# Second chunk's triangles out and back during the first solver, wider stages for the early weights, solver in slots 8 to 33, merges at slots 5 and 12

## The chip, the cores and the metric

The kernel runs on one core of a Trainium2 chip. The metric is the device time of one execution in microseconds (us). A core has five engines that each work through a list of their own in order: TensorE (PE in the profile, with its weight loads as PEld), VectorE (DVE), ScalarE (ACT), GpSimd (POOL) and SyncE (SP), which here does little but issue DMAs. An engine waits where its next instruction needs something that another engine or a DMA has not finished.

## The reference

Three layers follow one another. The first is a recurrence with a 40x40 state for each of 32 heads (4 batches x 8 heads) over 768 tokens; the other two are perceptrons over the 3072 tokens of its output.

```python
def _attn_ref(r, k, v, w, a, b):
    state = np.zeros((B, H, D, D)); y = np.zeros_like(r)
    for t in range(S):
        kt, vt, rt = k[:, :, t], v[:, :, t], r[:, :, t]
        wt, at, bt = w[:, :, t], a[:, :, t], b[:, :, t]
        y[:, :, t] = np.einsum('bhd,bhde->bhe', rt, state)
        Sa = np.einsum('bhde,bhe->bhd', state, at)
        state = state * wt[:, :, None, :] - np.einsum('bhd,bhe->bhde', Sa, bt) \
              + np.einsum('bhd,bhe->bhde', vt, kt)
    return y
...
x = attn_out.transpose(0, 2, 1, 3).reshape(3072, 320)
x = np.maximum(x @ w_in, 0.0) ** 2 @ w_out          # layer 0: 320 x 2048, 2048 x 320
h = x @ w_in2
out = (h * np.cos(h)) @ w_out2                       # layer 1
```

The perceptrons' weights arrive as 64-bit floats.

## The kernel before

**The recurrence in chunks.** The 768 tokens are cut into 12 chunks of 64. Within a chunk the recurrence becomes dense products with a triangular matrix of 64x64 per head, which must be inverted. `decay` makes the running products of `w`; `compact_kb` and `compact_a` lay k, b and a out; `gt` multiplies them on TensorE and VectorE masks the products into the tiles `ga`. `gt_out` writes the triangles in `ga` to DRAM (`Ls`, SyncE), `solve_load` fetches their diagonal blocks of 32x32 back, one per partition, into `L` (and the unit matrix `kti` into `T`), and `solve` inverts these 128 blocks: 31 steps of a product and a sum, 62 instructions, and a copy (line 517). I call this the **solver**; it runs on VectorE for chunk 0 and on GpSimd for the others. `solve_store` writes the result to DRAM (`Tn`, `Ts`), `load_t` fetches it in two layouts (`t_120`, which the trace shows as `t`, and `tt`), and `merge` joins the 32x32 blocks into 64x64 with products of `t`, `tt` and the corner block `l21` (loaded by `corner_load`; `l_119`, or `l`, in the trace): TensorE's `pw`, ACT's copy, `pt`, ACT's copy into `tt`, once for each half of the heads. `state` then runs a chunk's four groups of heads: `px` uses the triangles in `ga`, `pu` the merged `tt`, and the state goes on in `mov`, `mt` and `M0d`. In chunk 0, `pmat` fills parts of `mov` with zeros.

**The order.** It is written out by hand. `Program.run` writes the prologue, with chunk 0's solver on VectorE: a wrapper, `Vector`, puts one solver instruction behind each other instruction of VectorE while it has credit. Then `period(c)` is called for c = 0 to 11. A period is 42 slots; a table, `at(slot, function)`, says what is issued in which slot. Period c runs `state` of chunk c, the solver of chunk c + 1 (`rate[t]` of its instructions in slot t), and decay, layout and triangles of chunk c + 2. Each engine works in the order in which its instructions were issued, so the slot says who stands in front of whom on each engine; it says no time.

**The weights.** A 64-bit float is taken apart into two 32-bit words: ACT clamps (`clamp`), VectorE cuts the bits out (`bits`), GpSimd adds the low word (`add`, line 183, into `u`), and `split` makes a high and a low part on ACT and GpSimd (line 215, into `ws`). `first` does 12 early tiles of layer 0 whole (`w1`); a job's steps stand at numbered stages, and jobs start five stages apart. `rest` and `second` do the other tiles in `pieces` (`w2`, three for each tile) from period 2. The profile shows a step's tile by its number.

**The perceptrons.** Layer 0 is fed from period 2 on, a yield at a time, between the slots: `h` on TensorE, `g`, `gh` and `gl` on ACT and GpSimd (`gl` at line 766), `po` on TensorE. From about 863 us on there is only layer 1.

Of the kernel before, what the change touches and what calls it, by code (L numbers as in the profile page):

```python
# [158 lines left out]
class Weights:  # L159
# [58 lines left out]
    def first(self, last=NF, layer=0):  # L218
# [3 lines left out]
        def job(f):  # L222
# [9 lines left out]
            def begin(c0, n):  # L232
                u = st[c0] = m.p2.tile([128, 512], F32, tag="g", name="u1", bufs=3)[:, 0:n]
                if self.raw:
                    self.clamp(st["w"][:, c0:c0 + n], u)
                else:
                    self.nc.sync.dma_start(u, self.i[nm][f, :, c0:c0 + n])

            out = [(0, load)]
            for t, c0, n in ((5, 0, 384), (6, 384, DM)):  # L240
                out.append((t, lambda c0=c0, n=n: begin(c0, n)))
                if self.raw:
                    out += [(t + 1, lambda c0=c0, n=n: self.bits(st["w"][:, c0:c0 + n], st[c0])),
                            (t + 2, lambda c0=c0, n=n: self.add(st["w"][:, c0:c0 + n], st[c0], st[c0]))]
                out.append((t + 4, lambda c0=c0: self.split(st["dst"], st[c0], c0, layer)))
            return out
# [3 lines left out]
    def pieces(self, nm, tiles, period, end):  # L250
# [4 lines left out]
        def job(f, c0, n):  # L255
            st = {}

            def load():
                st["w"] = self.p.tile([128, 256, 2], I32, tag="w", name="w", bufs=2)[:, 0:n]
                self.load(nm, f, st["w"], c0)  # L260

            def clamp():
                st["u"] = self.p.tile([128, 256], F32, tag="u", name="u", bufs=2)[:, 0:n]
                self.clamp(st["w"], st["u"])

            return [(0, load), (4, clamp), (6, lambda: self.bits(st["w"], st["u"])),
                    (7, lambda: self.add(st["w"], st["u"], st["u"])), (period + 5, lambda: end(f, c0, st["u"]))]
# [40 lines left out]
class Attn:  # L308
# [274 lines left out]
    def pmat(self, c, g):  # L583
# [18 lines left out]
        for r0, n, s0 in ((64, 40, 0), (0, 64, 4)):  # L602
            if c:
                nc.scalar.activation(mov[r0:r0 + n, s0:s0 + 4, 64:104], self.MT[g][r0:r0 + n], AF.Copy)
            else:
                nc.gpsimd.memset(mov[r0:r0 + n, s0:s0 + 4], 0.0)

# [6 lines left out]

    def state(self, c, g):
        nc = self.nc
        ga, rv, mov = self.ga[c, g // 2], self.rv.pop((c, g)), self.mov.pop((c, g))
# [41 lines left out]
        if not last:  # L659
            self.vec.tensor_tensor(mt[0:104], yv[0:104, :, 64:104], mt[0:104], op=ALU.add)  # L660
        if c:
            self.vec.tensor_tensor(sz[0:104], yv[0:104, :, 0:64], sz[0:104], op=ALU.add)
        if not last:
            self.vec.tensor_tensor(mt[0:104], mt[0:104],
                                   self.lam[(c + 1) % 3][:, 4 * g:4 * g + 4, 64:65].to_broadcast([104, 4, 40]), op=ALU.mult)
        if g % 2 == 0:
# [282 lines left out]


FIRST, RATE = 9, 64.2 / 42


class Program:
# [59 lines left out]
    def run(self):  # L1014
# [57 lines left out]
        for k in range(10):  # L1072
            self.vec.credit = 6
            step(g1, 2 if k > 7 else 1)
            if k == 6:
                A.gt_out(1, 0, 0)
                A.gt_out(1, 0, 1)
            if k in (1, 3, 4, 5, 6, 7):
                step(self.w1)
# [24 lines left out]
    def period(self, c):  # L1104
# [9 lines left out]
        for half in range(2):  # L1114
            for k in range(5):
                for q in range(2):
                    at(20 * half + 4 * k, step, st[2 * half + q])
        for h, t0 in enumerate((5, 5) if c == 0 else (2, 2) if more else (4, 12)):
            mg = A.merge(h)
            at(t0, step, mg)  # L1120
            at(t0 + (4 if c and more else 2), step, mg)
        at(2, A.rv_load, c, 2)
        at(6, A.rv_load, c, 3)
        at(6, A.mov_load, c, 2)
        at(8, A.pmat, c, 2)
        at(14, A.mov_load, c, 3)
        at(16, A.pmat, c, 3)
        at(17, A.y_store, c, 0)
        at(37, A.y_store, c, 1)
        if more:  # L1130
# [9 lines left out]
            if c:  # L1140
                at(6, A.solve_load, c + 1)
            at(8 if c == 0 else 6, A.corner_load, c + 1)
            first, last = (2, 26) if c == 0 else (9, 36)
            for t in range(first, last):
                rate[t] = 3 if t % 3 == 0 or c == 0 else 2
            rate[last] = 100
            at(28 if c == 0 else 37, A.solve_store)
            at(30 if c == 0 else 38, A.load_t)
            at(23, A.rv_load, c + 1, 0)
# [138 lines left out]
```

## Time and profile before

| | |
|---|---|
| median of 3 runs | 1274.33 us (1273.46 to 1278.36) |
| the profiled execution: its time, its span | 1272.46 us, 1270.7 us |
| mean granted clock of TensorE | 0.916 |
| busy: PE, PEld | 1065.8 us (84%), 894.4 us (70%) |
| busy: DVE, ACT, POOL | 696.7 us (55%), 697.6 us (55%), 690.3 us (54%) |
| DMA | 115.96 MB, mean 91 GB/s |

The span is the time from the first instruction's start to the last one's end in the trace; the execution's own time is 1.76 us longer. Busy shares are means over stretches that have different limits, so they don't tell what bounds a stretch. In a row of the timeline the first number is the time from the start of the span, the second the duration; the operation, output and inputs follow, and a bracket at the end gives how long the engine was idle before the instruction and what ended that. A row with `SPq` is an issue in SyncE's queue, and its duration is that of issuing, not of the transfer.

### The profile page before, as it was taken

The numbers are of one execution on the slowest core, as the hardware profiler recorded it, in microseconds if no ns is written. First come the engines' busy times: TensorE is split into PE (matmuls) and PEld (weight loads), VectorE is DVE, ScalarE is ACT, GpSimd is POOL, SyncE is SP. The second block draws the span as 40 slices with busy tenths as digits, with TensorE's granted clock in tenths as the row PEclk, the third lists the DMA queues.
The fourth block names the chain that finished last, engine by engine and source line by source line (L and its number), as shares of the span: only waits on it lengthen the run. The fifth ranks groups of instructions, "written<-read, shape, count | busy, mean of one in ns | idle before, by whom it ended". The sixth has DMA issues, their size and how long they took to land.

```text
span 1270.7 us, 26720 instructions
## 1 busy us (share of the span) xinstructions
PE 1065.8 (84%) x10242; PEld 894.4 (70%) x10242; DVE 696.7 (55%) x1315; ACT 697.6 (55%) x1444; POOL 690.3 (54%) x1106
## 2 busy tenths in 40 slices
PE   3334636889889885989698989999999999999997
PEld 3334535667767764867577867777889999999996
DVE  7955964666657572666466634123696343443432
ACT  4223634566466554656456556547756555655553
POOL 3157693776638381838384838226796333333332
PEclk9996665888889897989799989999999999999999
DMA  8545726446372817463736362236101010101000
GB/s 197 126 100 144 178 82 123 104 97 150 60 172 64 166 44 160 101 140 73 167 92 145 69 133 74 59 99 210 68 19 46 1 47 1 47 9 38 1 21 24
DMA packets 267621, 115.96 MB, mean 91 GB/s; under 512 B 225036, under 2 KB 246028, under 8 KB 266652
## 3 DMA queue, kind: packets, MB, share of 16 engines
q1 hardware_dynamic: 265650, 113.47, 37.2%
q8 instruction: 83, 1.36, 0.4%
q10 hardware_dynamic: 1834, 0.69, 0.2%
q14 instruction: 54, 0.44, 0.1%
HBM read 88.42 MB, written 25.69 MB: 90 GB/s over the span
## 4 chain that ended last, share of the span: by engine, by line
PE 55%; POOL 18%; DVE 7%; DMA 7%; SPq 5%; issue 3%; ACT 3%; POOLq 0%; ACTq 0%; DVEq 0%
PE h L913 23%; PE pt L857 13%; PE po L867 9%; POOL T L513 5%; POOL ttmp L510 5%; DMA xf<-xs 3%; POOL gl L766 3%; POOL u L183 2%; PE pgt L459 2%; POOL ws L215 2%; DVE lam L146 2%; DVE u L146 1%; PE pu L644 1%; PE py L654 1%; DVE cin L146 1%
## 5 line engine op out<-in xcount | busy, mean ns | idle before, releaser
L913 PE MATMUL h<-xh,ws 128*128 128x512 f32 x960 | 328.8, 405 | 17.6 <-ACT g L763 17.0
L766 POOL TENSOR_TENSOR gl<-g,gh 128x512 fp32r<-128x512 f32 x96 | 126.0, 1313 | 201.5 <-ACT gh L765 150.4
L913 PE MATMUL h<-xl,ws 128*128 128x512 f32 x576 | 232.1, 403 | 0.2 <-DVE xl L146 0.2
L794 POOL TENSOR_TENSOR gl<-g,gh 128x512 fp32r<-128x512 f32 x96 | 125.1, 1303 | 190.9 <-ACT gh L793 161.5
L913 PEld LDWEIGHTS h<-xh,ws 128*128 128x128 f32 x960 | 182.4, 191 | 60.9 <-ACT g L763 21.6
L510 POOL TENSOR_TENSOR ttmp<-T,L 128x126 f32<-128x126 f32 (+22 forms) x310 | 123.6, 399 | 55.4 <-DMA L<-Ls 22.2
L867 PE MATMUL po<-gh,ws 128*128 128x512 f32 x480 | 142.9, 422 | 3.3 <-ACT o L813 2.7
L513 POOL TENSOR_TENSOR T<-T,ttmp 128x126 f32<-128x126 f32 (+22 forms) x310 | 132.1, 426 | 19.5
L857 PE MATMUL pt<-ws,gh 128*128 128x320 f32 x768 | 128.2, 309 | 0.5 <-DVE g L146 0.4
L763 ACT ACTIVATE g<-h 128x512 f32<-128x512 f32 x96 | 57.1, 594 | 129.5 <-PE h L913 106.8
L857 PEld LDWEIGHTS pt<-ws,gh 128*128 128x128 f32 x768 | 120.0, 188 | 8.3 <-DVE g L146 0.6
L913 PEld LDWEIGHTS h<-xl,ws 128*128 128x128 f32 x576 | 110.2, 191 | 20.7 <-DVE xl L146 1.4
L146 DVE SCALAR_TENSOR_TENSOR g<-n,h 128x512 f32<-128x512 int32 x96 | 65.9, 687 | 104.2 <-ACT n L774 101.7
L774 ACT ACTIVATE n<-h 128x512 int32<-128x512 f32 x96 | 57.3, 596 | 119.4 <-PE h L913 119.4
L146 DVE TENSOR_TENSOR mov<-pu,kc 64x416 f32<-64x416 f32 x96 | 56.5, 589 | 111.6 <-PE pu L645 99.1
L867 PEld LDWEIGHTS po<-gh,ws 128*128 128x128 f32 x480 | 93.4, 200 | 27.1 <-ACT o L813 3.3
L146 DVE TENSOR_TENSOR g<-g,h 128x512 f32<-128x512 f32 x96 | 65.8, 686 | 71.1 <-ACT g L778 71.0
L459 PE MATMUL pgt<-at,cin 40*128 40x104 f32 x768 | 71.0, 328 | 30.3 <-POOL at L439 12.8
L146 DVE TENSOR_SCALAR u<-u 128x160 f32<-128x160 f32 (+9 forms) x144 | 56.2, 391 | 64.0 <-ACT u L171 59.3
L459 PEld LDWEIGHTS pgt<-at,cin 40*128 40x128 f32 x768 | 61.5, 229 | 36.5 <-POOL at L439 13.5
L867 PE MATMUL po<-gl,ws 128*128 128x512 f32 x288 | 86.6, 405 | 0.0
L183 POOL TENSOR_TENSOR u<-u,w 128x384 int32<-128x384 int32 (+2 forms) x72 | 56.1, 779 | 53.7 <-DVE u L146 33.7
(112 smaller groups left out, 2310.3 us busy)
## 6 DMA issues: line engine op xcount, KB each, us to landing
w<-moe SPq DMA_DIRECT2D x20, 704.0 KB
rv<-rv SPq DMA_DIRECT2D x48, 256.0 KB
cin<-cin SPq DMA_DIRECT2D x8, 832.0 KB
Ls<-ga SPq DMA_DIRECT2D x48, 128.0 KB
L<-Ls SPq DMA_DIRECT2D x44, 128.0 KB
mov<-vt SPq DMA_DIRECT2D x96, 40.0 KB
xs<-yt SPq DMA_DIRECT2D x48, 80.0 KB
w<-moe SPq DMA_DIRECT2D x24, 160.0 KB
```

What stands on the lines that cost most here:

```text
L146: fn(*args, **kwargs)
L183: self.nc.gpsimd.tensor_tensor(t.bitcast(I32), u.bitcast(I32), w[:, :, 0], op=ALU.add)
L459: nc.tensor.matmul(pv[par][:, j], self.kb[r0:r0 + 40, p0 + j].rearrange("p h b -> p (h b)"), self.at[r0:r0 + 40, p0 + j], start=True, stop ...
L510: eng.tensor_tensor(tv, T[:, 0:r, j:j + 1].to_broadcast([128, r, n]), L[:, j:j + 1, j + 1:32].to_broadcast([128, r, n]), op=ALU.mult)
L513: eng.tensor_tensor(T[:, 0:r, j + 1:32], T[:, 0:r, j + 1:32], tv, op=ALU.add)
L763: nc.scalar.activation(g, h, AF.Relu)
L766: self.later.append((2, lambda: nc.gpsimd.tensor_tensor(gl, g, gh, op=ALU.subtract)))
L774: nc.scalar.activation(n, h, AF.Copy, bias=0.25, scale=float(np.float32(1.0 / (2.0 * np.pi))))
L794: nc.gpsimd.tensor_tensor(gl, g, gh, op=ALU.subtract)
L857: nc.tensor.matmul(self.pos[j][:, 0:DM], x[:, 128 * j:128 * j + 128], wo[:, DM * ws:DM * ws + DM], start=(f == 0 and x is gh and ws == 0), ...
L867: nc.tensor.matmul(self.pos[m], wo[:, 128 * ws:128 * ws + 128], x, start=(f == 0 and k in (0, 2, 4)), stop=(f == NF - 1 and k in (5, 6, 7)))
L913: nc.tensor.matmul(h, wi[:, ws], x[:, kt], start=(k == 0), stop=(k == 7))
```

## The change

It has six parts.

- `first`: the load of an early tile stands two stages later, `bits` and `add` one stage later, `split` four stages later. The first 384 columns of the 32-bit value go into a tile of the tag `gl` instead of `g`.
- `pieces`: the load of a piece stands one stage later.
- Prologue: `gt` of chunk 1 advances two steps per round from the start of chunk 0's solver, so that its last `ga` is made about half way through it. `gt_out` of chunk 1's second half and `solve_load(1)` are issued there and no longer behind `load_t`.
- The zero fills of `pmat` for groups 2 and 3 of chunk 0 go from GpSimd to VectorE.
- `state`: the multiplication of `mt` by the decay comes ahead of the sum for `y`.
- The table of a period: the solver in slots 8 to 32 at 8 instructions in 3 slots, the remainder in 33 (before: 9 to 35 at 7 in 3, the remainder in 36), its stores and loads in 34 and 36 (37 and 38); merges at 5 and 12, three slots between the two halves of each (2 and 2 with four slots between; in period 0 5 and 5); the first two groups' `state` steps at 0, 4, 10, 14 and 18 (0, 4, 8, 12, 16), `load_kb` in 6 (1), and several loads and layouts a few slots later.

```diff
@@ first
-                u = st[c0] = m.p2.tile([128, 512], F32, tag="g", name="u1", bufs=3)[:, 0:n]
+                if c0 == 0 and self.raw:
+                    u = st[c0] = m.p2.tile([128, 512], F32R, tag="gl", name="u0", bufs=3).bitcast(F32)[:, 0:n]
+                else:
+                    u = st[c0] = m.p2.tile([128, 512], F32, tag="g", name="u1", bufs=3)[:, 0:n]
...
-            out = [(0, load)]
+            out = [(2, load)]
...
-                    out += [(t + 1, lambda c0=c0, n=n: self.bits(st["w"][:, c0:c0 + n], st[c0])),
-                            (t + 2, lambda c0=c0, n=n: self.add(st["w"][:, c0:c0 + n], st[c0], st[c0]))]
-                out.append((t + 4, lambda c0=c0: self.split(st["dst"], st[c0], c0, layer)))
+                    out += [(t + 2, lambda c0=c0, n=n: self.bits(st["w"][:, c0:c0 + n], st[c0])),
+                            (t + 3, lambda c0=c0, n=n: self.add(st["w"][:, c0:c0 + n], st[c0], st[c0]))]
+                out.append((t + 8, lambda c0=c0: self.split(st["dst"], st[c0], c0, layer)))
@@ pieces
-            return [(0, load), (4, clamp), (6, lambda: self.bits(st["w"], st["u"])),
+            return [(1, load), (4, clamp), (6, lambda: self.bits(st["w"], st["u"])),
@@ pmat
-                nc.gpsimd.memset(mov[r0:r0 + n, s0:s0 + 4], 0.0)
+                (nc.gpsimd if g < 2 else self.vec).memset(mov[r0:r0 + n, s0:s0 + 4], 0.0)
@@ state (the same multiplication of mt stood behind the sum into sz)
+            self.vec.tensor_tensor(mt[0:104], mt[0:104],
+                                   self.lam[(c + 1) % 3][:, 4 * g:4 * g + 4, 64:65].to_broadcast([104, 4, 40]), op=ALU.mult)
         if c:
             self.vec.tensor_tensor(sz[0:104], yv[0:104, :, 0:64], sz[0:104], op=ALU.add)
@@ run
-            step(g1, 2 if k > 7 else 1)
-            if k == 6:
+            step(g1, 2)
+            if k == 4:
                 A.gt_out(1, 0, 0)
                 A.gt_out(1, 0, 1)
+            if k == 7:
+                A.gt_out(1, 1, 0)
+                A.gt_out(1, 1, 1)
+                A.solve_load(1)
...
         A.solve_store()
         A.load_t()
-        A.gt_out(1, 1, 0)
-        A.gt_out(1, 1, 1)
-        A.solve_load(1)
@@ period
-                    at(20 * half + 4 * k, step, st[2 * half + q])
+                    at(t, step, st[2 * half + q])
-        for h, t0 in enumerate((5, 5) if c == 0 else (2, 2) if more else (4, 12)):
+        for h, t0 in enumerate((5, 12)):
...
-            at(t0 + (4 if c and more else 2), step, mg)
+            at(t0 + 3, step, mg)
...
-            first, last = (2, 26) if c == 0 else (9, 36)
+            first, last = (2, 26) if c == 0 else (SOLVE, END)
             for t in range(first, last):
-                rate[t] = 3 if t % 3 == 0 or c == 0 else 2
+                rate[t] = 2 if c and t % 3 == 0 else 3
             rate[last] = 100
-            at(28 if c == 0 else 37, A.solve_store)
-            at(30 if c == 0 else 38, A.load_t)
+            at(28 if c == 0 else END + 1, A.solve_store)
+            at(30 if c == 0 else END + 3, A.load_t)
...
-                at(1, A.load_kb, c + 2)
+                at(6, A.load_kb, c + 2)
```

How the instructions stand is shown at two places of SyncE's queue. The first is the prologue, from the loads of chunk 1's inputs to those that period 0 uses. `Ls<-ga` is `gt_out`, `lent<-kti` and `lent<-Ls` are `solve_load`, `Tn` and `Ts` are `solve_store`, `t_120` and `tt` are `load_t`, `w_...<-moe` is an early tile's load. Before:

```order
L473 DMA Ls<-ga 64x8x64 x2
L187 DMA w_419<-moe 128x1408
L524 DMA Tn<-L 64x512
L526 DMA Ts<-T 1024x1x32 x2
L533 DMA t_120<-Tn 32x32x16 x2
L539 DMA tt<-Ts 32x16x32 x4
L473 DMA Ls<-ga 64x8x64 x2
L493 DMA lent<-kti 128x512
L496 DMA lent<-Ls 32x32x32 x4
L573 DMA rv<-rv 128x512 x2
```

Now:

```order
L187 DMA w_378<-moe 128x1408
L476 DMA Ls<-ga 64x8x64 x4
L496 DMA lent<-kti 128x512
L499 DMA lent<-Ls 32x32x32 x4
L527 DMA Tn<-L 64x512
L529 DMA Ts<-T 1024x1x32 x2
L536 DMA t_120<-Tn 32x32x16 x2
L542 DMA tt<-Ts 32x16x32 x4
L187 DMA w_504<-moe 128x1408
L576 DMA rv<-rv 128x512 x2
```

The second half of chunk 1's triangles and their way back moved ahead of the stores of chunk 0's solver, and an early weight tile moved from ahead of these stores to behind `load_t`.

The second place is between two solvers on GpSimd, at the turn from period 3 to period 4, from the end of one `load_t` to the next `solve_load`. `cin<-cin` is `load_kb`, `mov<-vt` is `mov_load`, `T<-kti` and `L<-Ls` are `solve_load`. Before:

```order
L473 DMA Ls<-ga 64x8x64
L187 DMA w<-moe 128x320
L379 DMA cin<-cin 104x2048
L573 DMA rv<-rv 128x512
L187 DMA w<-moe 128x320
L473 DMA Ls<-ga 64x8x64 x2
L573 DMA rv<-rv 128x512
L581 DMA mov<-vt 64x4x40 x2
L493 DMA T<-kti 128x512
L496 DMA L<-Ls 32x32x32 x4
L501 DMA l_119<-Ls 32x16x32 x2
```

Now:

```order
L187 DMA w<-moe 128x256
L476 DMA Ls<-ga 64x8x64
L187 DMA w<-moe 128x320
L576 DMA rv<-rv 128x512
L476 DMA Ls<-ga 64x8x64 x2
L187 DMA w<-moe 128x320
L576 DMA rv<-rv 128x512
L584 DMA mov<-vt 64x4x40 x2
L496 DMA T<-kti 128x512
L499 DMA L<-Ls 32x32x32 x4
L382 DMA cin<-cin 104x2048
```

`cin<-cin` moved from ahead of the triangles' store to behind their load, and `l_119<-Ls` left this stretch for a later one.

## Rows read from the trace of the kernel before

**Rows 1.** Table of stretches: window, length, engines' busy us (instructions), PEclk, DMA share, GB/s.

```profile
410.00:476.00 66.00, 56.74 (x709) 45.02 (x707) 41.59 (x87) 36.47 (x83) 42.08 (x77) 0.95 0.47 104
476.00:546.00 70.00, 55.99 (x700) 45.52 (x701) 34.61 (x68) 39.18 (x88) 39.58 (x76) 0.88 0.53 118
863.00:1271.00 408.00, 398.79 (x2149) 356.29 (x2148) 198.24 (x281) 233.64 (x388) 190.01 (x165) 0.99 0.12 41
```

**Rows 2.** Waits of PE, 340 to 810: for whom, total us, count, longest.

```profile
PE pw L550 <- DMA t<-Tn: 37.8, 14, 9.2
PE pu L644 <- ACT tt L567: 14.9, 4, 7.4
```

**Rows 3.** Timeline of PE: the first product of two successive merges.

```profile
416.23 0.28 PE L550 MATMUL pw<-t,l 32*32 32x32 f32 x2 [5.14 <-DMA t<-Tn]
481.48 0.28 PE L550 MATMUL pw<-t,l 32*32 32x32 f32 x2 [9.22 <-DMA t<-Tn]
```

**Rows 4.** Timeline of POOL: first products and closing copies of solvers.

```profile
77.17 0.24 POOL L510 TENSOR_TENSOR lent<-lent 128x31 f32<-128x31 f32 x1 [22.01 <-DMA lent<-Ls]
...
114.76 1.34 POOL L517 COPY lent<-lent 64x512 f32<-64x512 f32 x1
...
146.21 0.24 POOL L510 TENSOR_TENSOR ttmp<-T,L 128x31 f32<-128x31 f32 x1 [0.52 <-DMA L<-Ls]
...
200.31 1.05 POOL L517 COPY L<-T 64x512 f32<-64x512 f32 x1
...
409.81 1.13 POOL L517 COPY L<-T 64x512 f32<-64x512 f32 x1
...
435.69 0.27 POOL L510 TENSOR_TENSOR ttmp<-T,L 128x31 f32<-128x31 f32 x1 [4.96 <-DMA l<-Ls]
...
474.90 1.31 POOL L517 COPY L<-T 64x512 f32<-64x512 f32 x1
...
795.72 1.12 POOL L517 COPY L<-T 64x512 f32<-64x512 f32 x1
```

**Rows 5.** Timeline of SyncE's queue between the solvers of chunks 5 and 6.

```profile
419.01 0.35 SPq L379 DMA_DIRECT2D cin<-cin  x1
...
419.87 1.52 SPq L473 DMA_DIRECT2D Ls<-ga  x2
...
429.36 3.95 SPq L496 DMA_DIRECT2D L<-Ls  x4
```

**Rows 6.** Timeline, prologue: end of the first solver, and the issue behind it.

```profile
60.25 0.59 DVE L517 COPY L<-T 64x512 f32<-64x512 f32 x1
...
66.68 2.26 SPq L473 DMA_DIRECT2D Ls<-ga  x2
```

**Rows 7.** Timeline of DVE: two sums of the first solver.

```profile
42.97 0.92 DVE L513 TENSOR_TENSOR T<-T,ttmp 128x126 f32<-128x126 f32 x1
...
46.79 0.29 DVE L513 TENSOR_TENSOR T<-T,ttmp 128x126 f32<-128x126 f32 x1
```

**Rows 8.** Groups of POOL, 60 to 116: count, busy us, mean ns, idle before.

```profile
L215 POOL TENSOR_TENSOR ws<-u,ws 128x256 fp32r<-128x256 f32 (+2 forms) x8 | 4.3, 555 | 0.0
L183 POOL TENSOR_TENSOR u<-u,w 128x320 int32<-128x320 int32 (+1 forms) x4 | 3.9, 962 | 0.0
L606 POOL MEMSET mov<- 40x416 f32 (+1 forms) x4 | 1.8, 455 | 0.2
```

**Rows 9.** Timeline of DVE, period 0: first `pu` product and last `ga` of chunk 2.

```profile
81.91 1.21 DVE L146 TENSOR_TENSOR mov<-pu,kc 64x416 f32<-64x416 f32 x2 [11.78 <-PE pu L645]
...
135.42 1.06 DVE L146 TENSOR_TENSOR ga<-pgt,kc 128x416 f32<-128x416 f32 x2
```

**Rows 10.** Groups of POOL within one solver run, 435.7 to 476.2.

```profile
L766 POOL TENSOR_TENSOR gl<-g,gh 128x512 fp32r<-128x512 f32 x6 | 7.7, 1276 | 0.0
L183 POOL TENSOR_TENSOR u<-u,w 128x160 int32<-128x160 int32 (+2 forms) x3 | 1.8, 606 | 0.0
```

**Rows 11.** Waits of all engines, 200 to 870: ACT for pieces of weights.

```profile
ACT u L171 <- DMA w<-moe: 6.3, 4, 3.7
```

More of the change, by code (lines that the diff above doesn't have):

```diff
@@ L660, in state @@
             self.vec.tensor_tensor(mt[0:104], yv[0:104, :, 64:104], mt[0:104], op=ALU.add)
+            self.vec.tensor_tensor(mt[0:104], mt[0:104],
+                                   self.lam[(c + 1) % 3][:, 4 * g:4 * g + 4, 64:65].to_broadcast([104, 4, 40]), op=ALU.mult)
         if c:
             self.vec.tensor_tensor(sz[0:104], yv[0:104, :, 0:64], sz[0:104], op=ALU.add)
-        if not last:
-            self.vec.tensor_tensor(mt[0:104], mt[0:104],
-                                   self.lam[(c + 1) % 3][:, 4 * g:4 * g + 4, 64:65].to_broadcast([104, 4, 40]), op=ALU.mult)
         if g % 2 == 0:
@@ L947, in step @@
             break
+SOLVE, END = 8, 33
 FIRST, RATE = 9, 64.2 / 42
@@ L1114, in period @@
         for half in range(2):
-            for k in range(5):
+            for t in (20, 24, 28, 32, 36) if half else (0, 4, 10, 14, 18):
                 for q in range(2):
-                    at(20 * half + 4 * k, step, st[2 * half + q])
-        for h, t0 in enumerate((5, 5) if c == 0 else (2, 2) if more else (4, 12)):
+                    at(t, step, st[2 * half + q])
+        for h, t0 in enumerate((5, 12)):
             mg = A.merge(h)
             at(t0, step, mg)
-            at(t0 + (4 if c and more else 2), step, mg)
+            at(t0 + 3, step, mg)
         at(2, A.rv_load, c, 2)
@@ L1124, in period @@
         at(6, A.mov_load, c, 2)
[L1125 to L1128, printed above, removed]
+        at(9, A.pmat, c, 2)
+        at(16, A.mov_load, c, 3)
+        at(19, A.pmat, c, 3)
+        at(19, A.y_store, c, 0)
         at(37, A.y_store, c, 1)
@@ L1141, in period @@
                 at(6, A.solve_load, c + 1)
-            at(8 if c == 0 else 6, A.corner_load, c + 1)
-            first, last = (2, 26) if c == 0 else (9, 36)
+            at(17, A.corner_load, c + 1)
+            first, last = (2, 26) if c == 0 else (SOLVE, END)
             for t in range(first, last):
-                rate[t] = 3 if t % 3 == 0 or c == 0 else 2
+                rate[t] = 2 if c and t % 3 == 0 else 3
             rate[last] = 100
-            at(28 if c == 0 else 37, A.solve_store)
-            at(30 if c == 0 else 38, A.load_t)
+            at(28 if c == 0 else END + 1, A.solve_store)
+            at(30 if c == 0 else END + 3, A.load_t)
             at(23, A.rv_load, c + 1, 0)
@@ L1158, in period @@
             if not A.ahead(c + 2):
-                at(1, A.load_kb, c + 2)
+                at(6, A.load_kb, c + 2)
                 at(11, A.load_a, c + 2)
             ck = A.compact_kb(c + 2)
-            for t in (3, 5, 7, 10) if c == 0 else (10, 12, 14, 16):
+            for t in (3, 5, 7, 10) if c == 0 else (16, 17, 19, 21):
                 at(t, step, ck)
-            at(20, A.compact_a, c + 2, 0)
+            at(22, A.compact_a, c + 2, 0)
             at(28, A.compact_a, c + 2, 1)
@@ L1172, in period @@
             self.dcs[c + 3] = A.decay(c + 3)
-            at(18, A.load_w, c + 3)
+            at(23, A.load_w, c + 3)
             if A.ahead(c + 3):
@@ L1179, in period @@
         for t in range(42):
-            if more and t == 9 and c:
+            if more and t == SOLVE and c:
                 self.solver = A.solve(A.nc.gpsimd)
```

## The prediction, made before the changed kernel was run

> **What bounds the kernel now.** I read the table of stretches first, then what TensorE waited for, then the start and end of each solver on GpSimd, then SyncE's queue between two solvers. Times "at" are microseconds from the start of the profiled execution.
>
> The stretches [rows 1]: from 863 to the end TensorE is busy 398.79 of 408.00 us. That part is second-layer work which the change leaves alone, so it costs the same again; only what lies before it can move. Between 410 and 546 TensorE idles 9.3 of 66 and 14.0 of 70 us. The waits [rows 2] name the idling: between 340 and 810, 37.8 us in 14 waits of the first merge for `t<-Tn`, the solved triangles coming back from DRAM, and 14.9 us in 4 waits of `pu` for ACT's copy of the merged triangles. The pair of rows for one period [rows 3]: merging begins at 416.23, and the next period's merge has to wait from 481.48 - 9.22 = 472.26. So TensorE's own work of one period takes 56.0 us, and the rest is waiting for the solver.
>
> Why does the solver come late? Its starts and ends [rows 4] form a ring. Chunk 5's ends at 409.81 + 1.13 = 410.94, chunk 6's starts at 435.69 and ends at 476.21. That is 24.75 us from end to start (I call it the **gap**) and 40.52 us from start to end (the **run**), together 65.3 us. From the end at 201.36 to the last at 796.84 nine such rings take 595.5 us, 66.2 each. No ring is shorter than its gap plus its run, since the next solver's triangles stand behind the last solver's stores in SyncE's queue; TensorE's 56.0 us fit inside. In the gap [rows 5] SyncE issues without pause until `Ls<-ga` has gone out at 421.39, yet `L<-Ls` goes out only at 429.36, when the former has landed, ends its issue at 433.31, and lands at 435.69. Ahead of `Ls<-ga` in the queue stands the transfer `cin<-cin` (104x2048 elements) at 419.01. So I cost the change by rings, not by TensorE's idle time.
>
> **The change part by part.**
>
> *Step 1, chunk 1's solver starts earlier.* It starts at 77.17, after 22.01 us of waiting [rows 4], because its `Ls<-ga` is issued at 66.68, behind the stores of the first solver, which VectorE ends only at 60.25 + 0.59 [rows 6]. Now the order has 31 of the first solver's 62 VectorE instructions behind the last `ga`; at 0.29 us [rows 7] that is 9 us, so the issue can come at about 52.5, 14 us earlier, and the start at about 63. After three solver instructions GpSimd meets `u_428`, whose bits stand on VectorE behind the copy and five scans; I take 1.3 us of waiting. Gain 12.7 us. The four zero fills of `mov` inside this run (1.8 us, [rows 8]) go to VectorE, which idles 11.78 us there [rows 9]. Chunk 1's end: 14.5 us earlier. What of it reaches chunk 2's start is another thing.
>
> A row on what may eat into it: the VectorE form of 128x126 takes 0.92 us at 42.97, where GpSimd adds at the same time, and 0.29 at 46.79 [rows 7]. The Trainium skill, "SBUF — State Buffer", section "Who interferes with whom", says that VectorE and GpSimd share one port pair under an exclusive lock, so that one of them stands still; the trace agrees in that row. Before, VectorE's scans after the first solver met an idle GpSimd, now they meet the second solver: 12 two-input instructions at up to 0.63 us would take 7.6 us of the 14.5 at chunk 1's end. The sum would then be some 5 us smaller (about 1236); I leave it out, as the next step caps the gain anyway.
>
> *Step 2, to chunk 2's start.* That start, 146.21, lies 30.1 us after the end at 116.10. It needs `Ls<-ga` of chunk 2, and that the `ga` which VectorE makes at 135.42, 53.5 us after it resumed at 81.91 [rows 9]. If those 53.5 us stay as they are, and VectorE resumes when the merged triangles are there (about 76, since ACT first waits for the third weight tile, loaded behind the triangles), the gain is 5 us after the two fills that VectorE now does. If the wider stages of the early weights, whose split now stands five stages behind the add instead of two, take the waits out of the 53.5 us, chunk 2's start follows chunk 1's end in full: 17 us with a slightly shorter gap. Neither shows in the trace. I take **12 us**, nearer the upper end, because ACT stood behind GpSimd's adds in most of that stretch; the bounds are 5 and 17.
>
> *Step 3, chunk 2's run.* 146.21 to 201.36. The order leaves one add and two subtracts fewer in it: 0.96 + 2 x 0.55 = 2.1 us [rows 8]; some waiting in its first steps may go too. **3 us**, bounds 0 and 5.
>
> *Step 4, the nine later runs.* 8/3 steps per slot instead of 7/3 end the solver some four slots sooner in the order. GpSimd's own work in it stays, but less foreign work lies between. Counted in the order over the nine runs: 8 `gl` fewer, 3 adds and a subtract fewer. 8 x 1.28 + 3 x 0.61 + 0.5 = **12.5 us** [rows 8, 10]. They fall into the gap, where GpSimd idles; were that cover gone they would cost the same again.
>
> *Step 5, the gaps.* `cin<-cin` moves behind `L<-Ls` in eight of them (the ninth has none). The queue gains two `mov` issues, hidden behind the landing of `Tn`, and before `Ls<-ga` two of `xs` and one `w` more in some: three at 0.35 to 0.76 us each, some 1.25 us, against the 0.35 of `cin`, so 0.9 more [rows 5]. What `Ls<-ga` gains in landing is unknown. Upper bound: the 8.0 us from 421.39 to 429.36 fall to the 2.4 us that `L<-Ls` takes from the end of its issue to the start it releases (433.31 to 435.69): 5.6 less 0.9, 4.7 us a gap. Lower bound: nothing, or a loss of 1, if other transfers hold it up. I take **2 us, 16 us** in all, between the ends.
>
> *Edits at nothing.* The merges move from slots 2 and 6 to 5 and 12; TensorE's count changes only in order, and half of the heads are used from slot 20 on. The load of a piece one stage later, `corner_load`, `compact`, `load_a` later: hidden while the ring binds. `MT` multiplied one instruction earlier: I estimate half a microsecond, one such VectorE instruction, off a chain that isn't the ring.
>
> *Sum.* 12 + 3 + 12.5 + 16 = 43.5 us at the last solver's end, and the 474 us behind that stay. The profiled execution took 1272.46 us (span 1270.7): 1229.0. The median of the runs is 1.9 above it: **1231 us**, with its own range of 1212 to 1250 from the bounds.
>
> **Rivals.**
>
> *SyncE's burst is no shorter* (step 5 gives nothing; the transfers before `Ls<-ga` still fill the DMA engines). For: eight transfers leave in those microseconds in either order. Against: the heaviest one is gone. 1231 + 16 = 1247, down to 1257 with a loss of 1 us a gap.
>
> *TensorE becomes the bound* because the ring shrinks more than I say. Floor: 56.0 us and, in every other ring, 3.7 us for `pu` (14.9 / 4): 57.9. Nine rings x (66.2 - 57.9) + 15 = 90 us: 1185, or about 1200 if only half the way from my ring is gone. Against: the gap would have to fall by 6 us.
>
> *It does not do what it says:* the gain of step 1 is stopped by VectorE's chain and the gaps grow by what the runs lose. About 1270.
>
> *Slower: ACT waits for late weights.* The load of each small piece is issued one stage later, three slots before ACT reads it, and ACT works in order: `g<-h` stands behind it, then TensorE. Four such pieces a period. It decides where ACT's waits add up to more than the 66.2 - 57.9 = 8.3 us of slack, 2.1 us a piece. At 5 us a piece: nine rings x (20 - 8.3) = 105, less 15 from the start; at 3.5 us: 9 x 5.7 - 15 = 36 us slower: 1310. Against: in the trace ACT waited for `w` only 4 times, 6.3 us in all, between 200 and 870 [rows 11], with loads one stage sooner.
>
> **How the numbers follow.** Forecast 0.58, burst no shorter 0.17, TensorE the bound 0.10, nothing 0.06, slower 0.09. The range 1198 to 1258 holds the forecast, the burst and part of the TensorE case, some 0.8. Half a per cent (6.4 us) is about what a measurement of this kernel tells from no change. Faster by more: 0.58 + 0.17 + 0.10 = 0.85; same 0.06; slower 0.09.
>
> **What would show it.** Step 1: chunk 1's first solver instruction near 63 and its copy near 102. Step 2: chunk 2's start near 134. Step 4: five or four `gl` in a run, runs of 37 to 42 us. Step 5: gaps of 20 to 24 us. TensorE's waits for `t<-Tn` may stay, since the ring is still longer than 56 us; were they gone while rings still take 60, the ring would not be what binds. Wrong is the whole account if ends of solvers come 40 us earlier and the end of the program does not.

## The result, and the profile after

| | before | after |
|---|---|---|
| time, median | 1274.57 us (1273.46 to 1278.36, 4 runs) | 1241.00 us (1240.38 to 1247.46, 4 runs) |
| profiled execution: time, span | 1272.46, 1270.7 us | 1240.58, 1238.5 us |
| granted clock, mean | 0.916 | 0.929 |

The ratio is 0.9743, with a 95% interval of 0.9705 to 0.9781: 2.6% faster, 33.6 us by the medians, where 43.3 us had been forecast (1231). The time lies in the forecast's own range (1212 to 1250).

The stretches after, with the columns of [rows 1]: the turn of chunk 6, of chunk 7, layer 1, and all nine rings from chunk 2's solver to the last.

```profile
387.98:449.95 61.97, 59.97 (x763) 46.79 (x762) 40.31 (x83) 39.62 (x92) 41.20 (x76) 1.00 0.53 113
449.95:512.10 62.15, 55.77 (x643) 43.23 (x643) 36.28 (x69) 34.77 (x77) 39.39 (x76) 0.89 0.59 133
830.00:1238.00 408.00, 399.78 (x2152) 356.72 (x2151) 198.62 (x281) 234.75 (x389) 190.47 (x165) 0.99 0.12 41
187.87:763.80 575.93, 522.00 (x6284) 404.93 (x6281) 351.66 (x695) 344.93 (x794) 371.02 (x710) 0.92 0.53 117
```

Layer 1 costs the same: in a stretch of 408 us TensorE is busy 399.78 us with 2152 products, before 398.79 with 2151. A ring takes 575.93 / 9 = 64.0 us where it took 66.2, and in it TensorE is busy 58.0 us. What TensorE and ScalarE waited for, 200 to 870 (for whom, total us, times, longest):

```profile
PE h L916 <- ACT g L766: 30.2, 11, 5.2
...
ACT u L171 <- DMA w<-moe: 23.9, 7, 5.6
...
ACT ga L482 <- DMA Ls<-ga: 16.3, 5, 10.0
...
PE pt L566 <- ACT l L557: 13.0, 9, 6.6
```

Both waits of [rows 2] are gone: none of `pw` for `t<-Tn`, none of `pu` for `tt`. In their place TensorE waits for ScalarE's `g` and `l`, and ScalarE for the transfers `w` and `Ls` (its waits for the tokens `xf` fell, from 25.8 to 11.8 us). The starts and ends of solvers on GpSimd, for [rows 4]:

```profile
59.02 0.24 POOL L513 TENSOR_TENSOR lent<-lent 128x31 f32<-128x31 f32 x1 [9.96 <-DMA lent<-Ls]
59.34 0.25 POOL L516 TENSOR_TENSOR lent<-lent 128x31 f32<-128x31 f32 x1
59.67 3.58 POOL L513 TENSOR_TENSOR lent<-lent 128x30 f32<-128x30 f32 x1
...
104.83 1.30 POOL L520 COPY lent<-lent 64x512 f32<-64x512 f32 x1
...
135.78 0.24 POOL L513 TENSOR_TENSOR ttmp<-T,L 128x31 f32<-128x31 f32 x1 [0.80 <-DMA L<-Ls]
...
186.80 1.07 POOL L520 COPY L<-T 64x512 f32<-64x512 f32 x1
...
448.83 1.12 POOL L520 COPY L<-T 64x512 f32<-64x512 f32 x1
...
473.23 0.24 POOL L513 TENSOR_TENSOR ttmp<-T,L 128x31 f32<-128x31 f32 x1 [2.90 <-DMA w2f<-u]
...
762.74 1.06 POOL L520 COPY L<-T 64x512 f32<-64x512 f32 x1
```

Chunk 1's solver starts 18.2 us sooner and ends only 10.0 sooner (106.13 for 116.10); chunk 2's ends 13.5 sooner (187.87), the last one 33.0 sooner (763.80 for 796.84). Behind it stand 474.7 us, for 473.9 before. So the whole gain lies in front of the last solver's end, as the account by rings had it. From such rows, for each of the nine rings, come runs and gaps. The next table has their sums, for every kernel of this study, with the ends of chunk 2's and of the last solver. All columns but the last come from one execution of each kernel; those of `e1_start` and `e4_merge_early` took 1268.4 and 1251.7 us, 5 us above their medians, so their runs and gaps are somewhat long.

| kernel | chunk 2 ends | nine runs | nine gaps | last ends | time, median |
|---|---|---|---|---|---|
| before | 201.4 | 373.2 | 222.3 | 796.8 | 1274.6 |
| after | 187.9 | 353.7 | 222.3 | 763.8 | 1241.0 |
| e1_start | 191.5 | 375.6 | 225.9 | 792.9 | 1263.5 |
| e2_table | 199.0 | 354.1 | 220.6 | 773.7 | 1252.4 |
| e3_kb_first | 187.5 | 351.0 | 248.7 | 787.1 | 1265.3 |
| e4_merge_early | 188.0 | 357.5 | 229.6 | 775.1 | 1246.7 |
| e5_short_all | 187.1 | 261.6 | 248.6 | 697.3 | 1184.1 |
| e6_first_back | 187.3 | 353.9 | 222.3 | 763.6 | 1240.5 |
| e7_short_one | 180.8 | 357.3 | 222.1 | 760.2 | 1238.4 |
| e8_x_late | 187.4 | 386.9 | 214.9 | 789.2 | 1268.3 |
| e9_ahead | 187.8 | 355.9 | 209.3 | 753.0 | 1231.1 |
| e10_rate_back | 189.6 | 377.4 | 194.5 | 761.5 | 1237.2 |
| e11_piece_back | 187.9 | 351.3 | 222.0 | 761.1 | 1240.2 |
| e12_ls_ahead | 187.2 | 356.6 | 202.1 | 745.9 | 1221.0 |

The change took 19.5 us off the runs (12.5 forecast) and nothing off the gaps (16 forecast). In SyncE's queue the gap of chunk 7, with the solver's end at 449.95 and the next start at 473.23, shows why:

```profile
449.97 0.49 SPq L527 DMA_DIRECT2D Tn<-L  x1
...
451.99 1.26 SPq L584 DMA_DIRECT2D mov<-vt  x2
...
456.80 0.81 SPq L613 DMA_DIRECT2D xs<-yt  x2
...
460.78 2.60 SPq L719 DMA_DIRECT2D xf<-xs  x4
463.48 1.31 SPq L476 DMA_DIRECT2D Ls<-ga  x2
...
466.82 0.60 SPq L496 DMA_DIRECT2D T<-kti  x1
467.53 3.26 SPq L499 DMA_DIRECT2D L<-Ls  x4
470.88 0.58 SPq L382 DMA_DIRECT2D cin<-cin  x1
```

`L<-Ls` now follows `T<-kti` at once. The wait for the landing of `Ls<-ga` no longer shows, but from the solver's end to `Ls<-ga` going out there is issue behind issue. I cut each gap at three points of this queue (last `Ls<-ga` out, first `L<-Ls` begun, last `L<-Ls` out) and added up the nine. The last column counts SyncE's pauses above 0.15 us:

| us in nine gaps | to `Ls<-ga` out | on to `L<-Ls` | issuing `L<-Ls` | landing | SyncE idle up to `L<-Ls`, about |
|---|---|---|---|---|---|
| before | 127.3 | 43.5 | 28.2 | 23.4 | 17 |
| after | 135.8 | 29.0 | 29.7 | 27.8 | 7 |
| e3_kb_first | 152.4 | 44.2 | 27.5 | 24.5 | 18 |
| e9_ahead | 123.8 | 29.6 | 30.4 | 25.5 | 16 |
| e10_rate_back | 108.6 | 28.3 | 29.5 | 28.1 | 2 |
| e12_ls_ahead | 115.9 | 31.4 | 29.5 | 25.3 | 13 |

After: 14.5 us gained behind `Ls<-ga`, 8.5 lost ahead of it, 5.9 lost in issuing and landing `L<-Ls`. That is the theory the runs below test: **a ring of GpSimd's run and SyncE's issues sets the end, and every issue that stands behind the solver's end and ahead of `L<-Ls` lengthens it.** The rivals are that TensorE (or ScalarE in front of it) sets the period by now, and that issues beside a landing count nothing.

### The profile page after: what moved, and what is told of

Its sections match the earlier page's. It is cut to its first block, busy times and chain, and to the rows that moved or that the text cites. A ratio compares the mean times of both kernels' runs of the same rounds, so it can differ in the third digit from the quotient of the medians.

```text
span 1238.5 us, 26726 instructions
## 1 busy us (share of the span) xinstructions
PE 1076.7 (87%) x10242; PEld 891.1 (72%) x10242; DVE 718.0 (58%) x1319; ACT 695.8 (56%) x1444; POOL 701.4 (57%) x1102
## 4 chain that ended last, share of the span: by engine, by line
PE 53%; POOL 19%; DVE 10%; DMA 6%; SPq 5%; issue 4%; ACT 3%; POOLq 0%; ACTq 0%; DVEq 0%
PE h L916 23%; PE pt L860 13%; PE po L870 8%; POOL T L516 5%; POOL ttmp L513 5%; DVE lam L146 3%; POOL gl L769 2%; POOL u L183 2%; DVE cin L146 2%; DVE u L146 2%; DMA L<-Ls 2%; POOL ws L215 2%; PE pu L648 1%; PE pgt L462 1%; DVE ga L146 1%
## 5 line engine op out<-in xcount | busy, mean ns | idle before, releaser
L916 PE MATMUL h<-xh,ws 128*128 128x512 f32 x960 | 333.0, 409 | 30.7 <-ACT g L766 30.2
L516 POOL TENSOR_TENSOR T<-T,ttmp 128x126 f32<-128x126 f32 (+22 forms) x310 | 131.1, 423 | 20.1
L870 PEld LDWEIGHTS po<-gh,ws 128*128 128x128 f32 x480 | 89.7, 193 | 24.7 <-ACT o L816 3.1
L183 POOL TENSOR_TENSOR u<-u,w 128x384 int32<-128x384 int32 (+2 forms) x72 | 59.0, 819 | 53.8 <-DMA Ls<-ga 23.4
L870 PE MATMUL po<-gl,ws 128*128 128x512 f32 x288 | 89.1, 406 | 0.1
L146 DVE TENSOR_TENSOR mov<-pp,kc 64x256 f32<-64x256 f32 x96 | 40.3, 420 | 80.3 <-PE pp L596 79.6
L781 ACT ACTIVATE g<-g,kc 128x512 f32<-128x512 f32 x96 | 69.7, 726 | 26.9 <-DVE g L146 25.8
```

Source lines behind the costliest of these rows:

```text
L146: fn(*args, **kwargs)
L183: self.nc.gpsimd.tensor_tensor(t.bitcast(I32), u.bitcast(I32), w[:, :, 0], op=ALU.add)
L516: eng.tensor_tensor(T[:, 0:r, j + 1:32], T[:, 0:r, j + 1:32], tv, op=ALU.add)
L781: nc.scalar.activation(g, g, AF.Sin, bias=self.kc[:, K_QT:K_QT + 1])
L870: nc.tensor.matmul(self.pos[m], wo[:, 128 * ws:128 * ws + 128], x, start=(f == 0 and k in (0, 2, 4)), stop=(f == NF - 1 and k in (5, 6, 7)))
L916: nc.tensor.matmul(h, wi[:, ws], x[:, kt], start=(k == 0), stop=(k == 7))
```

## Experiments

**The two halves of the change.** `e1_start` is the kernel before with the start alone changed, `e2_table` the changed kernel with its start put back:

```diff
 # e2_table, against the changed kernel (and first, pmat as before)
-            step(g1, 2)
-            if k == 4:
+            step(g1, 2 if k > 7 else 1)
+            if k == 6:
...
-            if k == 7:
-                A.gt_out(1, 1, 0)
-                A.gt_out(1, 1, 1)
-                A.solve_load(1)
...
+        A.gt_out(1, 1, 0)
+        A.gt_out(1, 1, 1)
+        A.solve_load(1)
```

> The kernel before with the start alone changed: chunk 1's triangles out and back during the first solver, the wider stages of the early weights, the zero fills on VectorE; the table of a period stays as before. If rings of solver run and SyncE burst set the end (theory), the 13.5 us by which chunk 2's solver ended sooner in the changed kernel (201.36 to 187.87) reach the end almost whole: 1274.5 - 13 = 1261. If TensorE's own chain sets it (rival), a sooner solver only waits longer for TensorE: 1270 to 1274.

> The changed kernel with its start put back, so the table of a period, the load stage of the pieces and the earlier product into mt alone. Theory (rings): nine rings were 19.6 us shorter in sum, so 1274.5 - 20 = 1254 or 1255, and with the start the two parts add up. Rival (the parts need each other, since TensorE binds as soon as one of them is in): 1245 or less, or above 1265.

Measured: 1263.5 us (ratio 0.991, 0.9882 to 0.9938) and 1252.4 (0.9834, 0.9806 to 0.9861), against 1274.2 beside them: 10.7 and 21.8 us off, 32.5 together, where the whole change gives 33.6. The parts add up and neither needs the other. `e1_start` keeps TensorE's waits of [rows 2] (36.8 and 20.1 us between 200 and 860) and is 10 us faster all the same, so a sooner solver does not just wait longer.

**Who sets the period.** `e5_short_all` leaves 16 of the 62 instructions out of nine solvers:

```diff
         for j in range(31):
+            if 3 <= self.nth <= 11 and 11 <= j < 19:
+                continue
```

> Leaves work out: in the solvers of chunks 3 to 11 the steps 11 to 18 of 31 are missing (16 of 62 instructions, 9.8 us of a run by the trace of the changed kernel), so the inverses are not the real ones. It asks who sets the period of 64.0 us now. If the ring of GpSimd's run and SyncE's burst does (theory), each of nine rings shrinks until TensorE binds at the 57.9 us of the prediction's second rival: about 9 x 6 = 55 us earlier, 1186; more than half of it at the least. If TensorE with ScalarE's waits sets it already (rival), the ends of solvers come sooner but the period stays, 1230 to 1241.

Measured: 1184.1 us. Its nine rings as one stretch, and TensorE's two longest waits from 190 to 860:

```profile
187.09:697.26 510.17, 487.74 (x6174) 380.72 (x6169) 337.96 (x681) 337.90 (x779) 302.13 (x565) 0.97 0.61 132
```

```profile
PE h L919 <- ACT g L769: 12.7, 6, 5.9
PE pt L569 <- ACT l L560: 7.3, 3, 6.1
```

The rings fall from 64.0 to 56.7 us (510.17 / 9): the last solver ends 66.5 us sooner, and the program 57 (what stands behind the last solver takes 485.5 us for 474.7). In the changed kernel TensorE is still held by the ring, though no row of its waits names the solver: the waits for `g` fall from 30.2 to 12.7 us and those for `l` from 13.0 to 7.3 when the runs get shorter. How the hold reaches ScalarE was not tried by itself; its waits for `Ls<-ga` (16.3 us in the rows after) are a path on which SyncE's queue could hold it. In this kernel TensorE is busy 95.6% of the stretch, so 56.7 us is near its floor, and near the 57.9 of the second rival. That shows in the gaps too: the runs lost 92.1 us, but the gaps grew by 26.3. SyncE pauses in them for 29.5 us where it paused for 7, and 12 of that stand ahead of `rv<-rv`, which waits for TensorE's `pq`.

**The transfer `cin<-cin`.** `e3_kb_first` puts one line back:

```diff
-                at(6, A.load_kb, c + 2)
+                at(1, A.load_kb, c + 2)
```

> The changed kernel with load_kb back in slot 1, so the cin transfer of 104x2048 stands ahead of Ls<-ga in SyncE's queue again, in eight gaps. If the transfer itself held up the landing of the triangles (as the prediction had it, 2 us a gap), 16 us slower: 1257. If SyncE's issuing alone fills the gap (rival), only the issue moves, 0.4 to 0.6 us a gap: 1244 to 1246, or no change that shows.

Measured: 1265.3 us, 24 slower than the changed kernel; the gaps are 26.4 us longer in all, 3.3 for each of eight. Its own issue takes 0.34 to 0.56 us. SyncE's queue in two gaps of this kernel:

```profile
337.59 0.36 SPq L382 DMA_DIRECT2D cin<-cin  x1
...
342.03 4.74 SPq L476 DMA_DIRECT2D Ls<-ga  x2
...
406.07 0.35 SPq L382 DMA_DIRECT2D cin<-cin  x1
...
407.41 1.51 SPq L476 DMA_DIRECT2D Ls<-ga  x2
...
412.98 0.33 SPq L496 DMA_DIRECT2D T<-kti  x1
415.25 2.98 SPq L499 DMA_DIRECT2D L<-Ls  x4
```

In the first gap the issue of `Ls<-ga` itself takes 4.74 us, behind `cin` and `xf`, for 1.31 in the changed kernel; in the second, without `xf`, it takes 1.51, and `L<-Ls` waits until 415.25 for the landing. So it is in all eight: the issue takes 3.7 to 4.7 us in the four gaps with `cin` and `xf`, and 1.3 to 1.7 in the four with `cin` alone. The slower issues make some 11 us of the difference, the longer way from there to `L<-Ls` 15 (44.2 for 29.0 in the table). So the big transfer did hold up the triangles, by more than the 2 us a gap of the forecast. This part of step 5 was right, and too small.

**The solver's slots.** `e10_rate_back` puts the solver back where it was and keeps the rest:

```diff
-SOLVE, END = 8, 33
+SOLVE, END = 9, 36
...
-                rate[t] = 2 if c and t % 3 == 0 else 3
+                rate[t] = 3 if t % 3 == 0 or c == 0 else 2
...
-            at(28 if c == 0 else END + 1, A.solve_store)
-            at(30 if c == 0 else END + 3, A.load_t)
+            at(28 if c == 0 else 37, A.solve_store)
+            at(30 if c == 0 else 38, A.load_t)
```

> The changed kernel with the solver back in slots 9 to 36 at 7 instructions in 3 slots and its stores and loads in 37 and 38; merges, load_kb and all else as changed. By step 4 of the prediction the nine runs hold 8 gl and 3 adds more, 12 us longer in all. But the stores now stand behind mov<-vt and xs<-yt in SyncE's queue instead of ahead of them, and if every issue in the gap counts, the gaps are 2.06 us shorter each, 18 us. Theory: runs + 12, gaps - 18, about 1235. Rival (issues beside the landing of Tn count nothing, so only the runs move): 1249 to 1253.

Measured: 1237.2 us (0.9698, 0.9659 to 0.9736), no slower than the changed kernel. The runs are 23.7 us longer, some 12 of it other work of GpSimd inside them and some 10 waits, nearly all of `gl` for ScalarE; the gaps are 27.8 us shorter, and more than `mov` and `xs` (18.5) explain. The same gap of chunk 7:

```profile
449.67 0.49 SPq L527 DMA_DIRECT2D Tn<-L  x1
...
451.68 0.62 SPq L476 DMA_DIRECT2D Ls<-ga  x1
...
461.98 1.31 SPq L476 DMA_DIRECT2D Ls<-ga  x2
...
466.02 3.11 SPq L499 DMA_DIRECT2D L<-Ls  x4
```

Without `mov` and `xs` in it, and with one `Ls<-ga` already beside the landing of `Tn`, the gap takes 22.72 us for 23.28; before chunks 6, 8 and 10, without `xf`, it takes 19 for 23. Over the nine gaps six issues of weights are missing as well (21 for 27). What the earlier slots take off a run they put into the gap.

**The issues by themselves.** `e9_ahead` keeps the solver's new slots and moves four issues ahead of its stores:

```diff
-            at(34, A.mov_load, c + 1, 1)
+            at(33, A.mov_load, c + 1, 1)
-        at(37, A.y_store, c, 1)
+        at(33, A.y_store, c, 1)
```

> The changed kernel with the two mov<-vt issues of mov_load(c + 1, 1) (slot 34) and the two xs<-yt issues of y_store(c, 1) (slot 37) moved to slot 33, ahead of the solver's stores in SyncE's queue. The prediction costed the two mov issues at nothing, since they lie beside the landing of Tn, and the two xs at part of 0.9 us a gap. If every issue in the gap counts (theory), the gaps shrink by 1.25 + 0.81 = 2.06 us each, nine of them 18 us: 1223. If the mov issues are hidden (the prediction), 0.8 us a gap: 1234. If SyncE now waits at slot 33 for the buffers of TensorE and VectorE (rival), no gain or a loss: 1241 or more.

Measured: 1231.1 us (0.9634, 0.9586 to 0.9683); gaps 13.0 us shorter, last solver 10.8 sooner. One gap:

```profile
503.65 0.77 SPq L613 DMA_DIRECT2D xs<-yt  x2
504.52 1.20 SPq L584 DMA_DIRECT2D mov<-vt  x2
510.06 0.49 SPq L527 DMA_DIRECT2D Tn<-L  x1
...
512.42 2.03 SPq L536 DMA_DIRECT2D t<-Tn  x2
515.75 1.89 SPq L542 DMA_DIRECT2D tt<-Ts  x4
```

The four are out before the solver ends, and SyncE now idles for the landing of `Tn` and `Ts` (before 512.42 and 515.75): 7 us in nine gaps, for less than 1 in the changed kernel, out of 16 that it idles in all. Eight gaps are like this one, and 13.7 us shorter in sum: of 16.5 us of issues most counted, and the rest lay beside a landing. In the ninth, chunk 5's, `xs` waits for VectorE until the solver has ended, the stores stand behind it for 3.2 us, and the gap is 0.7 longer, as the rival had it. That is between the theory and the prediction, nearer the theory.

`e12_ls_ahead` adds the first half of the triangles to what goes ahead of the stores:

```diff
-            for t in (24, 25, 26, 32, 33, 34, 36, 37, 38):
+            for t in (24, 25, 26, 29, 30, 31, 36, 37, 38):
...
-            at(37, A.gt_out, c + 2, 0, 0)
-            at(39, A.gt_out, c + 2, 0, 1)
+            at(33, A.gt_out, c + 2, 0, 0)
+            at(33, A.gt_out, c + 2, 0, 1)
```

> The kernel of the run before with mov and xs ahead of the stores, and in addition the first half of chunk c + 2's triangles ahead of them too: the second quarter of its products in slots 29 to 31 instead of 32 to 34, both Ls<-ga issues of that half in slot 33 instead of 37 and 39. Two issues of 1.3 us leave each gap. If every issue in the gap counts (theory), nine gaps lose 10 to 12 us beside the run with mov and xs ahead, which took 1231: 1220. If the landing of Tn, for which SyncE idled 16 us in the nine gaps of that run, takes the place of the issues, or the wait for ga holds up the stores (rival): 1229 to 1233.

Measured: 1221.0 us (0.9549, 0.9514 to 0.9583 of the kernel before). The gaps are 7.2 us shorter again, less than the 10 to 12 expected (in chunk 5's the stores now stand back 4.5 us), and the last solver's copy stands at

```profile
744.75 1.13 POOL L520 COPY L<-T 64x512 f32<-64x512 f32 x1
```

This version is faster than both kernels: 20 us ahead of the changed one, with the same arithmetic.

**A load moved out of the gap at another's cost.** `e8_x_late`:

```diff
-            if c % 2 == 0 and c and t == 2:
+            if c % 2 == 0 and c and t == (2 if c == 2 else 7):
...
-            if c % 2 == 0 and t == (FIRST - 3 if c == 2 else 5):
+            if c % 2 == 0 and t == (FIRST - 3 if c == 2 else 10):
```

> The changed kernel with the four issues of xf<-xs (load_x of a block of tokens, 2.6 us of SyncE's queue in every second gap) moved behind the load of the next solver's triangles, slot 2 to 7 in periods 4 to 10, and the block released to layer 0 at slot 10 instead of 5. If the gap is SyncE's issuing (theory), the four gaps concerned shrink by 2 to 3 us each, 8 to 12 us in all: 1229 to 1233. If TensorE, which gets its next block five slots later, is the bound (rival), the end does not move or moves out: 1241 to 1250.

Measured: 1268.3 us, 27 slower. The gaps did shrink, by 7.4 us in all, but four runs grew by 6 to 9 us each. The chain in one of them, on ScalarE, TensorE and GpSimd:

```profile
485.94 0.63 ACT L733 ACTIVATE xh<-xf 128x512 fp32r<-128x512 f32 x1 [10.71 <-DMA xf<-xs]
...
488.79 0.79 PE L916 MATMUL h<-xh,ws 128*128 128x512 f32 x1 [7.12 <-ACT g L766]
...
490.13 1.27 POOL L769 TENSOR_TENSOR gl<-g,gh 128x512 fp32r<-128x512 f32 x1 [7.24 <-ACT gh L768]
```

ScalarE waits 10.71 us for the tokens, `gh` is late, and the `gl` that stands between two solver instructions holds the solver up for 7.24 us. Neither theory had this: a run is not GpSimd's own work alone, since everything that was put between its instructions waits in order.

**The merges, the early weights, chunk 1's run and the pieces.**

```diff
 # e4_merge_early
-        for h, t0 in enumerate((5, 12)):
+        for h, t0 in enumerate((5, 5) if c == 0 else (2, 2) if more else (4, 12)):
...
-            at(t0 + 3, step, mg)
+            at(t0 + (4 if c and more else 2), step, mg)
 # e6_first_back: load, bits, add and split of first at stages 0, 1, 2, 4 and the tag g, as before
 # e7_short_one: as e5_short_all, for chunk 1's solver alone
+            if 1 <= self.nth <= 1 and 11 <= j < 19:
+                continue
 # e11_piece_back
-            return [(1, load), (4, clamp), (6, lambda: self.bits(st["w"], st["u"])),
+            return [(0, load), (4, clamp), (6, lambda: self.bits(st["w"], st["u"])),
```

> The changed kernel with the merges back in slots 2 and 6 (5 and 7 in period 0). Theory (rings of GpSimd and SyncE): TensorE waits for t<-Tn again, some 25 to 40 us in all, runs and gaps keep their lengths, and the end moves by less than 5 us: 1241 to 1246. Rival (the gain of the changed kernel is the merges' place, since TensorE no longer stands at them): 1255 or more.

Measured: 1246.7 us (0.978, 0.9753 to 0.9807). TensorE waits for `t<-Tn` again, 15.9 us, fewer than expected. The interval overlaps that of the changed kernel, and the trace (gaps 7.3 us longer) is of an execution of 1251.7, the longest of the four: at most some 6 us for the merges, and whether that is more than nothing stays open. It is not where the gain comes from.

> The changed kernel with the stages of the early weights as before (load 0, bits 1, add 2, split 4 stages; tile from the tag g). Theory (the wide stages take ScalarE's and VectorE's waits out of period 0, so chunk 2's solver can follow): chunk 2's first solver instruction 5 to 8 us later than at 135.8, end 1246 to 1249. Rival (VectorE's chain follows the first solver anyway, the stages do nothing): start of chunk 2 within 1 us, end within 2 us of 1241.

Measured: 1240.5 us. Chunk 2's solver starts at

```profile
137.30 0.24 POOL L510 TENSOR_TENSOR ttmp<-T,L 128x31 f32<-128x31 f32 x1
```

1.5 us later than at 135.78, and ends 0.6 sooner: the wide stages do nothing for the time.

> Leaves work out: chunk 1's solver alone lacks its steps 11 to 18 (16 instructions, some 10 us), so its inverse is not the real one. It gives back what chunk 1's run lost beside VectorE (38.9 us before, 47.1 in the changed kernel). If chunk 1's end sets chunk 2's start through SyncE's queue, where a weight tile and the stores stand behind it (theory), chunk 2's start comes 7 to 10 us sooner and the end too: 1231 to 1234. If VectorE's chain up to the last ga of chunk 2 sets it (rival, as the prediction's step 2 had it in its lower bound), less than 2 us: 1239 to 1241.

Measured: 1238.4 us. Chunk 1's last copy and chunk 2's first instruction:

```profile
95.31 1.03 POOL L523 COPY lent<-lent 64x512 f32<-64x512 f32 x1
...
128.92 0.24 POOL L516 TENSOR_TENSOR ttmp<-T,L 128x31 f32<-128x31 f32 x1 [0.90 <-DMA L<-Ls]
```

Chunk 1 ends 9.8 us sooner than in the changed kernel and chunk 2 starts 6.9 sooner, so chunk 1's end does carry over to chunk 2. But only 3.6 us are left at the last solver and 2.6 at the end, less than these medians tell apart: the runs take 3.6 us more, with waits of some 5 us in them for 1.

> The changed kernel with the load of a piece of the late weights at stage 0 again, one stage earlier. ScalarE waited for these pieces 7 times, 23.9 us, between 200 and 870 in the changed kernel, and 4 times, 6.3 us, before. If these waits fall on slack of ScalarE (theory), they go and the end stays within 3 us of 1241. If they hold up g, h and the solver's runs through gl, as the last rival of the prediction had it, the end comes 8 us or more sooner: 1233 or less.

Measured: 1240.2 us, with ScalarE's waits between 200 and 870 at

```profile
ACT u L171 <- DMA w<-moe: 10.3, 3, 4.7
```

for 23.9 in the changed kernel. The later load does make ScalarE wait, and the waits cost nothing that shows. They also move on in part: ScalarE's waits for `Ls<-ga` are 29.1 us here, for 16.3.

## Why the prediction was right, point by point

- **What binds** was right, and `e5_short_all` shows it for the changed kernel too. One of its tests was wrong: "were they gone while rings still take 60, the ring would not be what binds". TensorE's waits for `t<-Tn` did go and the rings take 64.0 us, yet the ring binds; the waiting only moved to `h` and `pt`.
- **Step 1**, 12.7 us and 1.8 for the fills: the start came 18.2 us sooner, the end 10.0 instead of 14.5. Chunk 1's run grew from 38.9 to 47.1 us. The 128x30 product at 59.67 takes 3.58 us, where in the kernel before it took 0.24, while VectorE makes the first solver's copy and its scans (59.66 to 63.22). The Trainium skill, "SBUF — State Buffer", section "Who interferes with whom", says that the two engines share a port pair under an exclusive lock and one stands still while the other has it; the trace agrees in that row. Yet that row is not where the run lost its time, for the next instruction on GpSimd has to wait for VectorE in any case: for the bits of a weight tile, which VectorE has ready at 64.45, just ahead of the `lam` that the row names. In `e6_first_back` the same product takes 0.24, the wait behind it 6.01, and the run 47.5 us. One row of the changed kernel, then two of `e6_first_back`:

```profile
64.60 1.50 POOL L183 TENSOR_TENSOR u<-u,w 128x384 int32<-128x384 int32 x1 [1.35 <-DVE lam L146]
```

```profile
60.09 0.24 POOL L510 TENSOR_TENSOR lent<-lent 128x30 f32<-128x30 f32 x1
66.34 1.13 POOL L183 TENSOR_TENSOR u<-u,w 128x320 int32<-128x320 int32 x1 [6.01 <-DVE lam L146]
```

So the wait for these bits cost the changed kernel 1.35 + 3.34 (3.58 less 0.24) = 4.7 us, where the prediction took 1.3; the solver's other instructions, beside VectorE, took about 3 us more than before. The prediction named a further loss of 7.6 us, put it down to the port, and left it out of the sum.

- **Step 2**, 12 us: 10.4. The reason was the wrong one of the two: `e6_first_back` shows that the wide stages give nothing. The gap from chunk 1's end is as long as before (29.65 for 30.11), and chunk 1's end came 10.0 us sooner. By `e7_short_one` about 7 of 10 us at that end reach chunk 2's start.
- **Step 3**, 3 us: 3.1 (55.15 to 52.09).
- **Step 4**, 12.5 us: the other work inside the nine runs fell by 11.6 us, as counted. Nearly all the rest came from waits inside the runs (10.7 us before, 1.2 after; rows overlap a little, so the two parts add up to more than 19.5), which the prediction did not look for. In `e10_rate_back` they come back with the old slots. But the step asked only what leaves the run; what enters the gap with the earlier stores was left to step 5.
- **Step 5**, 16 us, is the step that failed: the gaps gave nothing. Two things in it were mis-sized. The wait ahead of `L<-Ls` was read from one gap, [rows 5], with 8.0 us the longest of nine whose mean is 43.5 / 9 = 4.8; still, taking `cin` away was worth more than the 2 us a gap put down for it, since together with `xf` it also slowed the issue of `Ls<-ga`: 26.4 us in all by `e3_kb_first`. And "two `mov` issues, hidden behind the landing of `Tn`", at nothing, with the two of `xs`, part of 0.9 us a gap, cost 13 us (`e9_ahead`); with all else that the solver's earlier slots do to the queue it is 27.8 (`e10_rate_back`). 26.4 gained and 27.8 lost are about the zero, if they add up; no run puts both back.
- **Edits at nothing**: the pieces' load is at nothing, shown; the merges are at 6 us or less, open; `mt` was not tried.
- **Rivals**: the first, SyncE's burst no shorter (1247), describes the gaps as they came out, but not why. TensorE as the bound did not come; by `e5_short_all` its floor is about where the prediction had it. The slower case came in its first half, ScalarE's waits rising from 6.3 to 23.9 us ([rows 11]), and without its price.

In sum, at the last solver's end: 13.5 us for 15 at the start, 19.5 for 12.5 in the runs, 0 for 16 in the gaps: 33 for 43.5. That the time lies in the forecast's range and not at the 1247 of the first rival is in part luck: the waits inside the runs, which no step had in view, made up 7 of the 16 us that the gaps did not give.

## What to carry to other kernels

Where two engines hand a ring to each other, cost a move on both: work that an earlier slot takes out of one engine's stretch stands in the other's, and here the exchange of 24 us for 28 gained nothing. In a queue that issues without pause most of what is issued behind the hand-over counts (13.7 of 16.5 us here), so move what needs no hand-over ahead of it (20 us here), and read a wait from all its occurrences, not from the one that shows it best. An engine's waits can vanish while the same ring still sets its pace; only a run that shortens the ring tells.

## What the runs showed of the hardware

Transfers ahead in the queue can slow not only the landing of what follows but its issue: two `Ls<-ga` went out in 4.74 us behind `cin` and `xf`, in 1.31 behind `xf` alone and in 1.51 behind `cin` alone. So in these gaps it took both, and even that is no rule: in the kernel before, three of the four gaps with both show 3.7 to 5.0 us and one 1.31. One 128x30 product on GpSimd took 3.58 us beside VectorE's copy and scans, 15 times its 0.24 us in the kernel before, and cost nothing by itself, since the next instruction had to wait for VectorE anyway.
